# An attention and two expert layers on one core: where in SBUF the matmul operands lie, modulo 256 bytes

## The chip, the cores and the metric

The kernel runs on one core of one Trainium2 chip. The metric is the device time of one execution in microseconds (us). Three executions of the kernel before took 971.79, 973.72 and 978.30 us, median 973.72; the profiled execution took 974.34 us, of which its span from the first to the last instruction is 972.5 us, so 1.8 us lie around the span.

An SBUF address below is a byte offset inside a partition. "Residue" means that address modulo 256. For a pair of matmuls that follow each other, "offset" means the residue of the second one's weights (the stationary operand) less the residue of what the first one streams (the moving operand), modulo 256: it compares the two reads that TensorE makes at the same time.

## The reference

```python
def phi(x):                                  # q, k: (4, 8, 576, 64), omega: (128, 64)
    h = einsum('bhsd,md->bhsm', x, omega) - sum(x * x, -1) / 2
    return exp(h - max(h)) / sqrt(128)
kv, z = einsum('bhsm,bhsd->bhmd', phi(k), v), sum(phi(k), 2)
attn = einsum('bhsm,bhmd->bhsd', phi(q), kv) / (einsum('bhsm,bhm->bhs', phi(q), z) + 1e-6)
x = attn as (2304, 512)
x = (silu(x @ w_gate) * (x @ w_val)) @ w_out          # 512 -> 1536 -> 512, first expert layer
h = x @ w_in                                          # 512 -> 2048, second expert layer
g = where(h >= 1, h, where(h <= -1, 0, (h + 1)**2 / 4))
return g @ w_out2                                     # 2048 -> 512
```

All of it is float32; the expert weights arrive as 64-bit floats.

## The kernel before

**Products.** Each large product is made of three TensorE products of a high and a low part of both operands, so that 128x128 weights are loaded and 256 columns streamed three times for one result (`split3`, lines 397 to 400): L398 streams the high part, L399 the low part past the same weights, L400 the high part past the low part of the weights. 7,134 of the program's 7,782 matmuls stand on these three lines. Each tile that such a product reads holds the high part and, 2,048 bytes or a multiple of it behind, the low part, so both have one residue.

**Stages.** Up to about 250 us the attention runs (lines 605, 678, 763, 867, 875), mixed with the first steps of the first expert layer (`moe1`). From there to about 600 us the rest of the first expert layer runs, and after 600 us the second one. In both layers PE alternates between a few products of an *up* projection (`set_up`, `tail_up`: streamed is x, weights are w) and a few of a *down* projection. In the first layer's down projection (`out1`, `down1`) the activations `hl` are streamed past the weights; in the second layer's (`down2`, `down_end`) the activations `hl` are the stationary operand, and the weights `w` are streamed.

**Order.** A planner in the kernel (class `Planner`) simulates the engines with fixed costs and writes the order of all instructions at build time. Buffers of one role form a `Ring`; a process takes one with `Get`, and `pl.put` gives it back. The planner doesn't know addresses.

**Homes.** Tiles get their addresses in the order in which the pools hand them out, and `pad` puts unused bytes between them. `wring` holds the weight slots: 9 of the pool `keep` (`w`), later 8 of `rb` (`wb`) and 7 of `wl` (`wx`). `hrow` holds the activation rows `hl` and `hlr`. `x1s` and `xur` hold what the up products stream.

| operand | names in the rows | residue before |
|---|---|---|
| x of up products | x1s, xur | 160 |
| weights, of up and of down products | w, wb, wx | 224 |
| activations of down products | hl, hlr | 160 |
| attention | omr, omh, oml 224; ki, qi, vi, ebk, ebq, qtn, kvr, xhl 64; qt, kvz, ids 192 | mixed |

So the offset of neighbouring matmuls is 64 inside the up products and through the whole first expert layer; inside the second layer's down products it is 192; where that layer goes from an up to a down product or back it is 0; in the attention it is 0, 32, 96, 128, 160 or 192, by the pair (qt with kvz 0, omh with xhl 96).

Of the kernel before, what the change touches and what calls it, by code (L numbers as in the profile page):

```python
# [42 lines left out]
SLACK_D, SLACK_U = 3.0, 0.8  # L43

SLACK_A = 0.0

NATK = 3

# [232 lines left out]
def performer_moe_kernel(ctx: ExitStack, tc: tile.TileContext, qG, kG, om, ident,  # L281
# [10 lines left out]
    def ring(*a):  # L292
        return Ring(bufs(*a))
# [4 lines left out]
    keep = ctx.enter_context(tc.tile_pool(name="keep", bufs=1, side="left"))  # L298
    acc = []
    bank = ring(psum, "bank", 8, [P, 512])  # L300
    def pad(pool, name, nbytes):
        pool.tile([P, nbytes // 4], F32, name=name)

    pad(keep, "pad0", 352)
    wring = ring(keep, "w", 9, [P, 2, 512], F32R)
    wstage = ring(keep, "ws", N_WS, [P, 1024], U32)
    wtmp = ring(keep, "wt", 2, [P, 512])
    half = keep.tile([P, 1], F32, name="half")
# [16 lines left out]
    att = att_cm.__enter__()  # L325
    ebufs = {False: ring(att, "ebk", EBK, [P, 512]), True: ring(att, "ebq", EBQ, [P, 512])}
    kin = ring(att, "ki", KINS, [P, 512])
    vin = ring(att, "vi", VINS, [P, 576])
    qin = ring(att, "qi", QINS, [P, 512])
    lent_cm = tc.tile_pool(name="lent", bufs=1, side="left", reuse_waits="tile")  # L330
    lent = lent_cm.__enter__()
    lent_ids = set()
# [19 lines left out]
    lend(vin, "vl", N_VL, [P, 576])  # L352
    lend(qin, "ql", 2, [P, 512])
    lend(ebufs[False], "el", 2, [P, 512])
    nat_b = sorted({b for b in range(4) for k in range(NATK) if b * 576 < (k + 1) * TB and k * TB < (b + 1) * 576})
    kvr = {(b, d): att.tile([P, 2, 2, P], F32, name=f"kvr{b}_{d}") for b in nat_b for d in range(2)}
    qts0 = ring(att, "qtn", 3, [P, 2, TB])
    xhl = ring(att, "xhl", 2, [P, 2, 256], F32R)
    stat = ring(att, "st", 10, [P, 4, 4])
    rec = ring(att, "rec", 2, [P, TB])  # L360
    qts = ring(att, "qt", N_QT, [P, 2, 2, TB], F32R)
    kvz = [[att.tile([P, 2, 2, 2, P], F32R, name=f"kvz{b}_{d}") for d in range(2)] for b in range(2)]
    ids = att.tile([P, P], F32, name="ids")
    rect = ring(att, "rect", 1, [P, TB // 32, 33])
    nc.gpsimd.memset(rect.free[0][0][:, :, 32:33], 1e-6)
    omr = att.tile([P, 256], F32, name="omr")
    omh = att.tile([P, 256], F32R, name="omh")
    oml = att.tile([P, 256], F32R, name="oml")


    def dma(dst, src, nbytes):
# [52 lines left out]
        pl.put(wstage, st)  # L424
        return t

    def conv_key(key, src, slot):
        st = yield Get(wstage)
        pl.set(wdone[key])
        t = yield from to_f32(st, src, None)  # L430
        yield from parts(slot[:, 0], slot[:, 1], t, 512)
        pl.put(wtmp, t)
        wslot[key] = slot
        pl.set(wready[key])

    def conv(key, src, rng, prio):
# [2 lines left out]
        pl.spawn(conv_key(key, src, slot), prio)  # L439
        yield wdone[key]  # L440

    def wfree(key, rng):
        pl.put(rng, wslot.pop(key))

    moe_on = Ev()
    NE = N_EARLY[0]
# [55 lines left out]
    def w_feed():  # L502
        for m, a, order, sets in passes:
            for c in sets:
                for s, p in columns(m, c):
                    slots, tt = [], []
                    for i in range(2):
                        yield staged[s, 2 * p + i]
                    for _ in range(2):
                        tt.append((yield Get(wt2)))  # L510
                    for _ in range(4):
                        slots.append((yield Get(wring)))
                    pl.spawn(conv_pair(s, p, tt, slots), PR_W)
                for key in set_keys(m, c)[4:]:
                    yield staged[key]
                    t = yield Get(wt2)
                    slot = yield Get(wring)
                    pl.spawn(conv_one(key, t, slot), PR_W)

    def late_rank():  # L520
        return PR_C if moe_on.done else PR_CS
# [11 lines left out]
    def conv_pair(s, p, tt, slots):  # L533

        hs = [pl.spawn(dma(tt[i], w32[s, 2 * p + i], 262144), 0.6) for i in range(2)]
        for h in hs:
            yield h
        t0, t1 = tt
        lo, hi = slice(0, 256), slice(256, 512)
        yield from conv_slot((s, 2 * p), t0, slots[0])  # L540
        yield from conv_slot((s, 2 * p + 1), t1, slots[1])
# [4 lines left out]
        yield from conv_slot(("c" + s, p), t1, slots[2])  # L546
        pl.put(wt2, t1)
        yield from conv_slot(("d" + s, p), t0, slots[3])
        pl.put(wt2, t0)


# [376 lines left out]
    def att_close():  # L928
        for k in range(NBLK):
            yield x1_ready[k]  # L930
        att_cm.__exit__(None, None, None)
        rb = ctx.enter_context(tc.tile_pool(name="rb", bufs=1, side="right", reuse_waits="tile"))
        for rng, name, n, c in ((xpart, "xr", N_XR, [P, 512]), (ebr, "eb", N_EB, [P, 512]), (gbr, "gb", N_GB, [P, 1024]),
                                (wt2, "wtr", N_WT, [P, 512]), (hbuf, "hbr", N_HB, [P, 512]), (xq, "xq", N_XI, [P, 512])):
            for t in bufs(rb, name, n, c):
                pl.put(rng, t)
        for rng, name, n, more in ((hrow, "hlr", N_HL, 320), (wring, "wb", NB1, 192)):
            for t in bufs(rb, name, n, [P, 2, 512], F32R):
                pl.put(rng, t)
# [3 lines left out]
        pad(rb, "pad5", 320)  # L943
        pl.set(right_b)
        LEAN["DVE"], LEAN["POOL"] = LEAN_B, POOL_B

# [44 lines left out]
    def row_out(row, h):  # L991
        if len(row) > 2:
            if row[2] is not None:
                yield row[2]
        hl = yield Get(hrow)
        if len(row) > 2:
            pl.set(row[3])
        yield from parts(hl[:, 0], hl[:, 1], h, 512)
        pl.put(hbuf, h)
        row[1].append(hl)  # L1000
        pl.set(row[0])

    def evac1(k, d, last):
# [76 lines left out]
    def out1(step, h_ev, res):  # L1080
        k, fp = step
        first, last, end = run[step]
        for i in range(2):
            yield wready["o", 2 * fp + i]
        yield h_ev
        ws = [wslot["o", 2 * fp + i] for i in range(2)]
        hl = res[0]
        for n in range(KD):
            d, c = divmod(n, 2)
            if first and c == 0:  # L1090
                yield acc_free[d]
# [8 lines left out]
        pl.put(hrow, hl)  # L1100
        for f in (2 * fp, 2 * fp + 1):
            if last_use[f] == step:
                wfree(("o", f), wring)
# [155 lines left out]
    for m, a, order, sets in passes:  # L1259
        for j in order:  # L1260
            for c in sets:
                n = 2 if m == 1 and j < 4 else 1 if m == 1 else 4 if j < 4 else 2
                for r in range(n):
                    rows[m, a, j, c, r] = Ev(), [], before, Ev(), got, Ev()
                    before, got = rows[m, a, j, c, r][3], rows[m, a, j, c, r][5]

    def relu(dst, src, n):
# [310 lines left out]
    def late_down():  # L1578
        yield moe1_v
        yield from out1(*pend1.pop())  # L1580
        for m, a, order, sets in passes:
            for j in order:
# [14 lines left out]
                for i, (k, f, cols, end) in enumerate(todo):  # L1597
# [7 lines left out]
                    else:  # L1605
                        yield from (down1 if m == 1 else down2)(a, j, f, res[0], cols, i == 0, i == len(todo) - 1)
                    if end:
                        pl.put(hrow, res[0])
# [12 lines left out]

# [98 lines left out]
```

## Time and profile before

| | |
|---|---|
| median of three executions | 973.72 us |
| profiled execution, its span | 974.34 us, 972.5 us |
| PE busy, of the span | 958.3 us, 99% |
| DVE busy | 825.9 us, 85% |
| ACT busy | 567.4 us, 58% |
| POOL busy | 96.4 us, 10% |
| granted TensorE clock | full speed in every slice (2.4 GHz) |
| PE share of the chain that ended last | 62% |

Matmuls overlap in the records: one takes some 0.28 us from its issue to its end, and the next begins after 0.11 to 0.12 us. So PE counts as busy all the time, and what tells its pace is the distance of two starts, the *pitch*: a stretch without a wait, divided by its matmuls. The count of a window holds those that began before it and reach into it as well, so 2.5 (0.28 over 0.113) are taken off a count before dividing.

### The profile page before, as it was taken

To read this page: it belongs to the slowest core of one execution; us is meant where nothing else is said; L and a number is where in the kernel's file an instruction comes from. 1 tells how busy PE (TensorE), PEld (TensorE's weight loads), DVE (VectorE), ACT (ScalarE), POOL (GpSimd) and SP (SyncE) were. 2 spreads that over 40 slices of the span, in tenths; PEclk is the share of its full clock that TensorE was granted. 3 is DMA by queue.
4 is the path that set the end of the run, shared out by engine and by line. 5 is a ranking of instruction groups with operands and counts; after the bars stand their busy time and mean duration, and the time that the engine had idled before them with its cause. 6 is when DMAs were issued, how large, how long until landed. Compare 5 with 4: busy or idle time off the path is not lost.

```text
span 972.5 us, 21171 instructions
## 1 busy us (share of the span) xinstructions
PE 958.3 (99%) x8094; PEld 939.7 (97%) x8094; DVE 825.9 (85%) x1695; ACT 567.4 (58%) x1490; POOL 96.4 (10%) x99
## 2 busy tenths in 40 slices
PE   8999999999999999999999999999999999999998
PEld 6789999999999999999999999999999999999998
DVE  7999899888999999999999899899788768866553
ACT  8999788878645645445454566564445455544331
POOL 0332337434300000000000000000000000000000
PEclk9999999999999999999999999999999999999999
DMA  8766656635568465573657653445313041303022
GB/s 300 254 199 189 196 157 220 198 132 174 177 215 266 135 230 186 186 266 126 202 193 241 224 197 120 131 136 202 131 55 120 1 141 45 130 6 106 1 88 87
DMA packets 90677, 154.67 MB, mean 159 GB/s; under 512 B 8528, under 2 KB 42320, under 8 KB 90576
## 3 DMA queue, kind: packets, MB, share of 16 engines
q1 hardware_dynamic: 90576, 153.32, 48.2%
q8 instruction: 63, 1.03, 0.4%
q14 instruction: 38, 0.31, 0.1%
HBM read 110.30 MB, written 42.99 MB: 158 GB/s over the span
## 4 chain that ended last, share of the span: by engine, by line
PE 62%; DVE 11%; DMA 7%; ACT 4%; issue 2%; SPq 1%; POOL 0%; DVEq 0%; POOLq 0%; ACTq 0%
PE bank L398 20%; PE bank L400 20%; PE bank L399 20%; DMA ws<-in_wo_dram 2%; PE bank L875 2%; DMA ws<-in_w_dram 2%; DMA xq<-x1d 1%; DVE x1s L391 1%; DVE wt L422 1%; DVE wt L420 1%; DVE gb L1289 1%; DVE hb L1281 1%; DMA ki<-in_kG_dram 1%; PE bank L763 1%; PE bank L678 1%
## 5 line engine op out<-in xcount | busy, mean ns | idle before, releaser
L398 PE MATMUL bank<-x1s,w 128*128 128x256 f32 x492 | 139.0, 283 | 0.3 <-ACT eb L379 0.3
L400 PE MATMUL bank<-x1s,w 128*128 128x256 f32 x492 | 137.0, 278 | 0.0
L399 PE MATMUL bank<-x1s,w 128*128 128x256 f32 x492 | 136.9, 278 | 0.0
L398 PEld LDWEIGHTS bank<-x1s,w 128*128 128x128 f32 x492 | 92.8, 189 | 0.6 <-ACT eb L379 0.5
L400 PEld LDWEIGHTS bank<-x1s,w 128*128 128x128 f32 x492 | 92.6, 188 | 0.0
L399 PEld LDWEIGHTS bank<-x1s,w 128*128 128x128 f32 x492 | 92.5, 188 | 0.0
L379 ACT ACTIVATE x1s<-xq 128x512 fp32r<-128x512 f32 x81 | 50.8, 628 | 54.5 <-PE bank L400 35.0
L398 PE MATMUL bank<-x1s,wx 128*128 128x256 f32 x278 | 78.3, 282 | 2.3 <-ACT eb L379 1.8
L398 PE MATMUL bank<-x1s,wb 128*128 128x256 f32 x286 | 79.9, 279 | 0.0
L399 PE MATMUL bank<-x1s,wb 128*128 128x256 f32 x286 | 79.7, 279 | 0.0
L400 PE MATMUL bank<-x1s,wb 128*128 128x256 f32 x286 | 79.7, 279 | 0.0
L400 PE MATMUL bank<-x1s,wx 128*128 128x256 f32 x278 | 77.6, 279 | 0.0
L399 PE MATMUL bank<-x1s,wx 128*128 128x256 f32 x278 | 77.5, 279 | 0.0
L379 ACT ACTIVATE eb<-bank 128x512 f32<-128x512 f32 x95 | 56.1, 591 | 26.5 <-PE bank L400 26.0
L415 ACT ACTIVATE wt<-ws 128x512 f32<-128x512 f32 x68 | 45.9, 678 | 42.2 <-DMA ws<-in_w_dram 22.9
L391 DVE TENSOR_TENSOR x1s<-xq,x1s 128x512 fp32r<-128x512 f32 x90 | 61.7, 686 | 7.8 <-ACT x1s L379 7.4
L379 ACT ACTIVATE hlr<-hb 128x512 fp32r<-128x512 f32 x53 | 33.4, 631 | 52.7 <-PE bank L399 39.0
L398 PEld LDWEIGHTS bank<-x1s,wx 128*128 128x128 f32 x278 | 52.5, 189 | 3.3 <-ACT eb L379 2.6
L624 DVE TENSOR_REDUCE st<-bank 128x4 f32<-128x512 f32 x72 | 48.8, 684 | 7.7 <-PE bank L605 3.5
L1289 DVE TENSOR_TENSOR gb<-bank,eb 128x512 f32<-128x512 f32 x64 | 43.9, 686 | 12.3 <-PE bank L400 11.9
L398 PEld LDWEIGHTS bank<-x1s,wb 128*128 128x128 f32 x286 | 54.0, 189 | 0.2 <-DVE eb L1289 0.2
L400 PEld LDWEIGHTS bank<-x1s,wb 128*128 128x128 f32 x286 | 53.8, 188 | 0.0
(281 smaller groups left out, 3629.3 us busy)
## 6 DMA issues: line engine op xcount, KB each, us to landing
ws<-in_w_dram SPq DMA_DIRECT2D x40, 512.0 KB, 4.8
ws<-in_wo_dram SPq DMA_DIRECT2D x28, 512.0 KB, 5.3
xq<-x1d SPq DMA_DIRECT2D x36, 256.0 KB, 4.8
xq<-x2d SPq DMA_DIRECT2D x36, 256.0 KB, 3.9
qi<-in_qG_dram SPq DMA_DIRECT2D x34, 256.0 KB, 3.2
ki<-in_kG_dram SPq DMA_DIRECT2D x33, 256.0 KB, 3.5
vi<-in_kG_dram SPq DMA_DIRECT2D x28, 192.0 KB, 3.4
x1d<-os SPq DMA_DIRECT2D x18, 256.0 KB, 3.2
```

Source lines behind the costliest of these rows:

```text
L379: yield Op("ACT", c_act(n), lambda: nc.scalar.activation(dst, src, AF.Copy, scale=1.0 if scale is None else scale))
L391: yield Op("DVE", c_dve(n), lambda: nc.vector.tensor_tensor(out=dst, in0=a, in1=b, op=op), True)
L398: nc.tensor.matmul(ps, l_hi, r_hi, start=first, stop=False, skip_group_check=shared)
L399: nc.tensor.matmul(ps, l_hi, r_lo, start=False, stop=False, skip_group_check=shared)
L400: nc.tensor.matmul(ps, l_lo, r_hi, start=False, stop=last, skip_group_check=shared)
L415: yield Op("ACT", 0.575, lambda: nc.scalar.activation(t, hw.bitcast(F32), AF.Abs))
L420: yield Op("DVE", c_dve(512), lambda: nc.vector.scalar_tensor_tensor(out=ti, in0=lw, scalar=29, in1=ti, op0=ALU.logical_shift_right, op1=A ...
L422: yield Op("DVE", c_dve(512), lambda: nc.vector.scalar_tensor_tensor(out=ti, in0=hw, scalar=0xC0000000, in1=ti, op0=ALU.bitwise_and, op1=A ...
L624: yield Op("DVE", c_dve(512), lambda: nc.vector.tensor_reduce(out=st[:, :, 0], in_=psv, axis=AX.X, op=ALU.max, negate=True))
L678: nc.tensor.matmul(kp[:, 2 * pr + a], e[:, u * P:(u + 1) * P], vb[:, vi + (dv if li == 4 else 0), a * 64:a * 64 + P], start=(li == 0 and a ...
L875: nc.tensor.matmul(ps[:, a, c0:c1], kz[:, l, r, a], q_t[:, h, a, c0:c1], start=(l == 0 and h == 0), stop=(l == 1), skip_group_check=True)
L1289: yield Op("DVE", c_dve(512), lambda: nc.vector.tensor_tensor(out=dst, in0=pq(ps), in1=pq(e), op=ALU.add))
```

## The change

No instruction is added, removed or moved: on each of the five engines the built program holds the same instructions in the same order with the same operands. What differs is the addresses, and the waits of seven instructions (one of SP's DMAs `xq<-x1d`, the first into the later right-hand pool, now also waits for the last matmul of L875; four other DMAs of SP and two DVE instructions lose one wait each).

Tiles are put in another order with other pads. A weight slot becomes 1,088 floats long instead of 1,024, and a process places its 1,024 inside by role (`split_at`): weights of up products, and the early weights of the first layer's down products, at the slot's start (residue 224); later weights of the first layer's down products (`"o"`) 32 floats in (residue 96); those of the second layer's (`"p"`) 48 floats in (residue 160). The activation rows become one tile with views; the second layer's begin 48 floats in (residue 96), those of the first layer at 160 as before.

| pair: streamed, then weights | offset before | offset after |
|---|---|---|
| up, up | 64 | 64 |
| first layer: down, down (late) | 64 | 192 |
| first layer: up, down; down, up | 64; 64 | 192; 64 |
| second layer: down, down | 192 | 192 |
| second layer: up, down; down, up | 0; 0 | 192; 64 |
| attention's pairs | 0 to 192, mixed | 64 |

The residue of what is streamed: before 160, and 224 in the second layer's down products; after 160 everywhere in the table.

```diff
+O_OFF, P_OFF, H_OFF = 32, 48, 48
...
+    def split_at(t, off):
+        return t[:, off:off + 1024].rearrange("p (h c) -> p h c", h=2)
...
-    pad(keep, "pad0", 352)
-    wring = ring(keep, "w", 9, [P, 2, 512], F32R)
+    wring, hrow = Ring([]), Ring([])
+
+    def slot_tiles(pool, name, n):
+        for t in bufs(pool, name, n, [P, 1088], F32R):
+            pl.put(wring, t)
+
+    def row_tiles(pool, name, n):
+        t = pool.tile([P, 1024 * n + 48], F32R, name=name)
+        for i in range(n):
+            v = t[:, 1024 * i:1024 * i + 1072]
+            pl.put(hrow, v)
+
+    pad(keep, "pad0", 32)
+    x1_sets = ring(keep, "x1s", 3, [P, 2, KD, TB], F32R)
+    row_tiles(keep, "hl", 2)
...
-    pad(keep, "pad1", 160)
-    x1_sets = ring(keep, "x1s", 3, [P, 2, KD, TB], F32R)
     hbuf = ring(keep, "hb", 3, [P, 512])
-    hrow = ring(keep, "hl", 2, [P, 2, 512], F32R)
...
+    pad(keep, "pad1", 96)
+    slot_tiles(keep, "w", 9)
...
-    def conv_one(key, t, slot):
+    def conv_one(key, t, raw):
         yield from dma(t, w32[key], 262144)
-        yield from conv_slot(key, t, slot)
+        yield from conv_slot(key, t, split_at(raw, O_OFF if key[0] == "o" else P_OFF))
+        whole[key] = raw
         pl.put(wt2, t)
...
+        def up(key, t, raw):
+            whole[key] = raw
+            return conv_slot(key, t, split_at(raw, 0))
...
-        for rng, name, n, more in ((hrow, "hlr", N_HL, 320), (wring, "wb", NB1, 192)):
-            for t in bufs(rb, name, n, [P, 2, 512], F32R):
-                pl.put(rng, t)
-            pad(rb, "pad" + name, more)
-        for t in bufs(rb, "xur", N_XU, [P, 2, 2, TB], F32R):
+        row_tiles(rb, "hlr", N_HL)
+        pad(rb, "padj", 64)
+        xur = bufs(rb, "xur", N_XU, [P, 2, 2, TB], F32R)
+        pad(rb, "padk", 64)
+        slot_tiles(rb, "wb", NB1)
...
-        hl = yield Get(hrow)
+        raw = yield Get(hrow)
+        hl = split_at(raw, H_OFF if len(row) > 2 and row[6] == 2 else 0)
...
-        pad(wl, "pad2", 320)
-        for t in bufs(wl, "wx", NWL, [P, 2, 512], F32R):
-            pl.put(wring, t)
+        slot_tiles(wl, "wx", NWL)
```

Left out above: the attention's tiles, which are created in another order with one pad of 64 bytes, and the lines that hand the whole slot back to its ring (`whole`, `raw`).

## Rows read from the trace of the kernel before

**Rows 1.** The page: busy time by engine; the chain that ended last, by engine.

```profile
PE 958.3 (99%) x8094; PEld 939.7 (97%) x8094; DVE 825.9 (85%) x1695; ACT 567.4 (58%) x1490; POOL 96.4 (10%) x99
...
PE 62%; DVE 11%; DMA 7%; ACT 4%; issue 2%; SPq 1%; POOL 0%; DVEq 0%; POOLq 0%; ACTq 0%
```

**Rows 2.** Stretches: from:to, length, then PE, PEld, DVE, ACT, POOL busy (xcount).

```profile
0.00:250.00 250.00, 243.69 (x1933) 227.58 (x1934) 220.01 (x581) 213.18 (x840) 89.50 (x93) 1.00 0.63 201
250.00:425.00 175.00, 172.17 (x1497) 170.54 (x1496) 163.22 (x314) 89.34 (x167) 6.85 (x6) 1.00 0.63 207
425.00:492.00 67.00, 67.00 (x570) 67.00 (x570) 65.14 (x126) 35.82 (x68) 0.00 (x0) 1.00 0.57 187
492.00:554.00 62.00, 60.76 (x533) 60.36 (x532) 56.31 (x107) 30.43 (x57) 0.00 (x0) 1.00 0.60 198
554.00:600.00 46.00, 45.82 (x389) 45.62 (x389) 45.81 (x88) 29.64 (x56) 0.00 (x0) 1.00 0.60 206
600.00:770.00 170.00, 170.00 (x1462) 170.00 (x1462) 146.50 (x266) 88.41 (x161) 0.00 (x0) 1.00 0.34 112
770.00:820.00 50.00, 50.00 (x440) 50.00 (x439) 35.49 (x61) 24.13 (x44) 0.00 (x0) 1.00 0.27 90
820.00:972.00 152.00, 148.83 (x1285) 148.63 (x1284) 93.37 (x158) 56.43 (x99) 0.00 (x0) 1.00 0.21 67
```

**Rows 3.** Two stretches of the first expert layer without a wait, same columns.

```profile
330.00:390.00 60.00, 60.00 (x532) 60.00 (x531) 57.83 (x112) 28.61 (x54) 0.00 (x0) 1.00 0.56 185
430.00:490.00 60.00, 60.00 (x512) 60.00 (x511) 58.18 (x114) 32.24 (x62) 0.00 (x0) 1.00 0.56 184
```

**Rows 4.** One form of matmul in 330 to 390 us, then in 425 to 492 us.

```profile
L399 PE MATMUL bank<-x1s,wb 128*128 128x256 f32 x28 | 7.7, 276 | 0.0
...
L399 PE MATMUL bank<-x1s,wb 128*128 128x256 f32 x40 | 11.2, 281 | 0.0
```

**Rows 5.** PE in order of time: the first matmul of five blocks of six.

```profile
860.46 0.28 PE L398 MATMUL bank<-wx,hl 128*128 128x256 f32 x1
...
861.14 0.28 PE L398 MATMUL bank<-xur,w 128*128 128x256 f32 x1
...
861.85 0.28 PE L398 MATMUL bank<-wx,hl 128*128 128x256 f32 x1
...
862.56 0.28 PE L398 MATMUL bank<-xur,wx 128*128 128x256 f32 x1
...
863.25 0.28 PE L398 MATMUL bank<-w,hlr 128*128 128x256 f32 x1
```

**Rows 6.** PE in order of time around a wait; in brackets the idle time and releaser.

```profile
492.50 0.28 PE L399 MATMUL bank<-x1s,wb 128*128 128x256 f32 x1
492.62 0.28 PE L400 MATMUL bank<-x1s,wb 128*128 128x256 f32 x1
493.76 0.39 PE L398 MATMUL bank<-x1s,wx 128*128 128x256 f32 x1 [0.86 <-ACT eb L379]
...
494.56 0.28 PE L398 MATMUL bank<-x1s,wb 128*128 128x256 f32 x1
...
494.90 0.28 PE L398 MATMUL bank<-x1s,wb 128*128 128x256 f32 x1
```

**Rows 7.** PE's waits in 250 to 600 us: total us, times, longest.

```profile
PE bank L398 <- ACT eb L379: 2.1, 5, 0.9
PE bank L399 <- DVE hlr L391: 0.6, 1, 0.6
PE bank L399 <- DVE hl L391: 0.6, 1, 0.6
PE bank L398 <- DVE eb L1289: 0.5, 1, 0.5
PE bank L398 <- ACT hl L379: 0.4, 1, 0.4
```

**Rows 8.** Two forms in 0 to 250 us, then L875's last matmuls and SP's DMA.

```profile
L400 PE MATMUL bank<-x1s,w 128*128 128x256 f32 x168 | 46.8, 279 | 0.0
...
254.77 1.60 PE L875 MATMUL bank<-qt,kvz 128*128 128x256 f32 x12
...
266.35 0.48 SPq L372 DMA_DIRECT2D xq<-x1d  x1
```

More of the change, by code (lines that the diff above doesn't have):

```diff
@@ L322, in performer_moe_kernel @@
     xpart = ring(keep, "xp", 2, [P, 512])
+    pad(keep, "pad1", 96)
+    slot_tiles(keep, "w", 9)
     att_cm = tc.tile_pool(name="att", bufs=1, side="right", reuse_waits="tile")
     att = att_cm.__enter__()
+    stat = ring(att, "st", 10, [P, 4, 4])
+    rec = ring(att, "rec", 2, [P, TB])
+    rect = ring(att, "rect", 1, [P, TB // 32, 33])
+    vin = ring(att, "vi", VINS, [P, 576])
+    qts0 = ring(att, "qtn", 3, [P, 2, TB])
+    qts = ring(att, "qt", N_QT, [P, 2, 2, TB], F32R)
+    ids = att.tile([P, P], F32, name="ids")
+    omr = att.tile([P, 256], F32, name="omr")
+    omh = att.tile([P, 256], F32R, name="omh")
+    oml = att.tile([P, 256], F32R, name="oml")
+    pad(att, "pada", 64)
     ebufs = {False: ring(att, "ebk", EBK, [P, 512]), True: ring(att, "ebq", EBQ, [P, 512])}
     kin = ring(att, "ki", KINS, [P, 512])
-    vin = ring(att, "vi", VINS, [P, 576])
     qin = ring(att, "qi", QINS, [P, 512])
+    nat_b = sorted({b for b in range(4) for k in range(NATK) if b * 576 < (k + 1) * TB and k * TB < (b + 1) * 576})
+    kvr = {(b, d): att.tile([P, 2, 2, P], F32, name=f"kvr{b}_{d}") for b in nat_b for d in range(2)}
+    xhl = ring(att, "xhl", 2, [P, 2, 256], F32R)
+    kvz = [[att.tile([P, 2, 2, 2, P], F32R, name=f"kvz{b}_{d}") for d in range(2)] for b in range(2)]
     lent_cm = tc.tile_pool(name="lent", bufs=1, side="left", reuse_waits="tile")
@@ L354, in performer_moe_kernel @@
     lend(ebufs[False], "el", 2, [P, 512])
[L355 to L364, printed above, removed]
     nc.gpsimd.memset(rect.free[0][0][:, :, 32:33], 1e-6)
-    omr = att.tile([P, 256], F32, name="omr")
-    omh = att.tile([P, 256], F32R, name="omh")
-    oml = att.tile([P, 256], F32R, name="oml")
     def dma(dst, src, nbytes):
@@ L425, in to_f32, with conv_key @@
         return t
-    def conv_key(key, src, slot):
+    def conv_key(key, src, raw):
+        whole[key] = raw
+        slot = split_at(raw, 0)
         st = yield Get(wstage)
@@ L440, in conv @@
         yield wdone[key]
+    whole = {}
     def wfree(key, rng):
-        pl.put(rng, wslot.pop(key))
+        del wslot[key]
+        pl.put(rng, whole.pop(key))
     moe_on = Ev()
@@ L516, in w_feed @@
                     t = yield Get(wt2)
-                    slot = yield Get(wring)
-                    pl.spawn(conv_one(key, t, slot), PR_W)
+                    raw = yield Get(wring)
+                    pl.spawn(conv_one(key, t, raw), PR_W)
     def late_rank():
@@ L526, in conv_slot @@
         pl.set(wready[key])
-    def conv_one(key, t, slot):
+    def conv_one(key, t, raw):
         yield from dma(t, w32[key], 262144)
-        yield from conv_slot(key, t, slot)
+        yield from conv_slot(key, t, split_at(raw, O_OFF if key[0] == "o" else P_OFF))
+        whole[key] = raw
         pl.put(wt2, t)
     def conv_pair(s, p, tt, slots):
+        def up(key, t, raw):
+            whole[key] = raw
+            return conv_slot(key, t, split_at(raw, 0))
         hs = [pl.spawn(dma(tt[i], w32[s, 2 * p + i], 262144), 0.6) for i in range(2)]
@@ L539, in conv_pair @@
         lo, hi = slice(0, 256), slice(256, 512)
-        yield from conv_slot((s, 2 * p), t0, slots[0])
-        yield from conv_slot((s, 2 * p + 1), t1, slots[1])
+        yield from up((s, 2 * p), t0, slots[0])
+        yield from up((s, 2 * p + 1), t1, slots[1])
         yield from two(t1[:, hi], t1[:, lo], t1[:, hi], 256, ALU.add)
@@ L545, in conv_pair @@
         yield from two(t0[:, hi], t0[:, hi], t0[:, lo], 256, ALU.subtract)
-        yield from conv_slot(("c" + s, p), t1, slots[2])
+        yield from up(("c" + s, p), t1, slots[2])
         pl.put(wt2, t1)
-        yield from conv_slot(("d" + s, p), t0, slots[3])
+        yield from up(("d" + s, p), t0, slots[3])
         pl.put(wt2, t0)
@@ L936, in att_close @@
                 pl.put(rng, t)
-        for rng, name, n, more in ((hrow, "hlr", N_HL, 320), (wring, "wb", NB1, 192)):
-            for t in bufs(rb, name, n, [P, 2, 512], F32R):
-                pl.put(rng, t)
-            pad(rb, "pad" + name, more)
-        for t in bufs(rb, "xur", N_XU, [P, 2, 2, TB], F32R):
+        row_tiles(rb, "hlr", N_HL)
[3 more added lines that the diff above has]
+        slot_tiles(rb, "wb", NB1)
+        for t in xur:
             pl.put(xu, t)
-        pad(rb, "pad5", 320)
         pl.set(right_b)
@@ L1000, in row_out @@
         row[1].append(hl)
+        row[1].append(raw)
         pl.set(row[0])
@@ L1099, in out1 @@
                 pl.spawn(evac1(k, d, end))
-        pl.put(hrow, hl)
+        pl.put(hrow, res[1])
         for f in (2 * fp, 2 * fp + 1):
@@ L1263, in performer_moe_kernel @@
                 for r in range(n):
-                    rows[m, a, j, c, r] = Ev(), [], before, Ev(), got, Ev()
+                    rows[m, a, j, c, r] = Ev(), [], before, Ev(), got, Ev(), m
                     before, got = rows[m, a, j, c, r][3], rows[m, a, j, c, r][5]
@@ L1607, in late_down @@
                     if end:
-                        pl.put(hrow, res[0])
+                        pl.put(hrow, res[1])
                     if j == order[-1]:
```

## The prediction

> **What bounds the kernel.** I read the page first: PE is busy 99% of the span and has 62% of the chain that ended last [rows 1]. The clock is granted in full throughout, so a gain has to come from the pitch of the matmuls, from start to start, or from PE's waits. I then cut the span into stretches [rows 2] and divided each by its matmuls, less the 2.5 that straddle a window's edges. There the reader should see two paces. In 330 to 390 us, 60 us hold 529.5 matmuls, a pitch of 113.3 ns; in 430 to 490 us they hold 509.5, a pitch of 117.8 ns [rows 3]. No PE idles in either, the instructions are the same forms, and all offsets in both are 64. I call these the short and the long pitch; one matmul of the same form takes 276 ns in the first and 281 ns in the second [rows 4], so the duration alone tells which pitch a group ran in.
>
> Two more views tell what sets the pitch. Where the streamed residue never changes (the first expert layer), the pitch is kept over hundreds of matmuls and changes at a wait of PE: before 493 us the starts are 0.12 us apart, then PE idles 0.86 us, and after it three matmuls take 0.34 us, 113.3 ns each [rows 6]. Where it does change (the second layer, 160 in up products, 224 in down products), blocks of six follow each other at 0.68, 0.71, 0.71 and 0.69 us [rows 5]: short, long, long, and one that begins long and ends short. So going from up to down keeps the pitch, going from down back to up flips it, and the layer runs half and half. Four blocks take 2.79 us, 116.3 ns a matmul; the windows of that layer say 116.5 (170.00 us over 1,459.5), 114.3 (50.00 over 437.5) and 116.1 (148.83 over 1,282.5) [rows 2].
>
> **The change, part by part.** Instructions added, removed or moved: none, so DVE, ACT, POOL and the DMAs keep their work. Of the seven waits that differ, the one that is new could matter, since everything behind it on SP's queue would be late: the DMA xq<-x1d is issued at 266.35 us, and the last L875 matmul that it must now await ends at 254.77 + 1.60 = 256.37 us [rows 8]. Ten us of slack: nothing. The six lost waits gain nothing either, for the same reason: they belong to tiles of the same closed attention pool.
>
> The offsets are what is left. After the change all that is streamed has one residue, 160, so the streamed side no longer jumps at the blocks' borders; only the weights alternate, at 64 and 192. Both offsets allow the short pitch: an up block at 64 and a down block at 192 both ran at 113.3 ns (0.68 us is six of them) [rows 3, 5]. What is unknown is whether a border between 64 and 192, without the jump, keeps the short pitch, and whether it ends the long one. No row shows such a border. The nearest are the borders of the second layer: from short, up to down keeps it; from long, down to up ends it within one block (0.69 us) [rows 5]. The border that turns short into long, down to up, does so while the streamed residue goes back from 224 to 160, which is gone. I therefore take it that the short pitch survives and that the long one is ended at some border; the other ends are the rivals.
>
> The terms, against the profiled execution's 974.34 us (0.62 above the median of 973.72, within the spread of the three times, so I use the result for the median as it is):
>
> - *Second expert layer, 600 to 972 us.* At 113.3 ns its 1,459.5 + 437.5 + 1,282.5 matmuls take 165.4 + 49.6 + 145.3 us instead of 170.0 + 50.0 + 148.8: 8.5 us less. It is on the path: PE idles nowhere there before its end, and DVE is busy 86%, 71% and 61% of the three windows. The middle window already runs close to the short pitch without a wait, so I take off only 0.4 us for waits that come up (0 to 2): 8.1.
> - *First expert layer, 250 to 600 us.* The long stretches are 425 to 492 and 554 to 600 us. At 113.3 ns their 567.5 and 386.5 matmuls would take 64.3 and 43.8 us, 2.7 and 2.2 less. But nearly all of the layer's waits of 4.2 us [rows 7] lie in the short stretches: PE idles 2.83 + 1.24 us in their 237 us and 0.00 + 0.18 us in the long ones [rows 2]. At that rate, 1.7%, the 113 us would lose 1.9 again: 3.0 is the upper end. The lower end is DVE, which is busy 65.14 of 67 and 45.81 of 46 us: if its work can't move, 1.9 + 0.2 = 2.1 are left. I take 2.5, between the two, which are near each other.
> - *Attention, 0 to 250 us.* All offsets become 64. L400's matmuls average 279 ns [rows 8], some 60% of the way from 276 to 281. If all 1,930 matmuls of the window gained 60% of 4.5 ns, that were 5.2 us; the lower end is zero, since PE idles 6.3 us there, and DVE (220 us) and ACT (213) are busy 88% and 85% and hold PE back. I take 1.0, near the lower end, because about half of these matmuls stream 256 columns in this way and the evictions that PE waits for don't get faster.
>
> Sum: 8.1 + 2.5 + 1.0 = 11.6 us, 974.34 - 11.6 = 962.7 us.
>
> **The rivals.**
>
> *The pitch keeps itself, the long one too.* If a border of 64 and 192 changes nothing in either direction, then each stretch keeps what the last wait left, as the first layer does now. The second layer has no waits, so it would run nearly whole in one pitch: short 974.3 - 8.5 = 965.8, long 3,179.5 x 117.8 ns = 374.5 instead of 368.8, 980.0 us. For it: the first layer's long runs at constant residues. Against: in the second layer a long block did end at a border, and alternating weights disturb the long pitch twice in twelve matmuls.
>
> *The short pitch is lost at the borders (slower).* If a border from 192 back to 64 turns short into long, as the one with the jump does now, and nothing turns it back, the second layer costs 5.7 us more, and the first layer's short stretches, 1,494.5 + 530.5 matmuls, 4.5 ns each, 9.1 us, of which the 4.1 us of waits in them are given back; with 1.0 in the attention 974.3 + 5.7 + 5.0 + 1.0 = 986 us. It decides once less than half of the second layer's blocks run short. For it: the flip in rows 5, and that the first layer's down products now alternate as well, which they did not. Against: the flip goes with a jump of the streamed side that no longer exists.
>
> *Addresses do nothing.* Then the two pitches have another cause (a neighbour's traffic, the moment a wait ends), and the time stays at 974, between 971 and 978. For it: both pitches occur at one and the same offset, 64 [rows 3], and they change at waits [rows 6]. Against: the strict pattern by blocks in the layer whose residues alternate [rows 5]. The Trainium skill speaks for this rival (SBUF — State Buffer, "Who interferes with whom"): TensorE's two read ports, one for the moving operand and one for the weights, are independent, and it waits on nobody. By that rule the sum would be zero; that equal forms without a wait run 4% apart in this trace shows only that something else than ports in that simple sense is at work.
>
> **The numbers.** The forecast has 0.64; the pitch that keeps itself 0.18, half of it short and half long; the short pitch lost 0.10; nothing 0.08. The predicted time is the forecast's, 962.7 us. Its own range is 957 to 968: 957 if the first layer gives its whole 4.9 and the attention 3, 968 if DVE eats the first layer's gain and the second layer gets waits of 2 us and a block in four stays long (0.03 us for each of some 130 blocks, 4 us, in part). To hold 8 times in 10 the range has to take in the rival without effect as well, up to 978; the long half of the first rival and the slower one are left out. 957 to 978 us.
>
> A change of 1%, 9.7 us, is about what a measurement of this kernel can tell from none. Below 964.0 lies some 0.7 of the forecast and a third of the short half of the first rival: 0.48 faster. Above 983.5 lies most of the slower rival: 0.08. The rest, 0.44, is within 1%.
>
> **What would show it.** In the profile after, matmuls of L398 to L400 should average 276 to 277 ns instead of 278 to 283, in the first layer and in the second. Five successive blocks of the second layer should start 0.68 us apart, all of them. The windows from 600 us on should hold the same 3,180 matmuls in some 360.5 us. The first layer's waits should grow to 5 to 6 us, and PE's share should fall a little below 99%. If the second layer's blocks show 0.71 throughout, the pitch kept itself or was lost; if they still alternate, the streamed residue was not the cause. If they are short, but the span shrinks by less than 8 us, PE met a wait that its slower pace hid, and that wait stands in the list of waits after 600 us, where there is none now.

## The result and the profile after

The changed kernel takes 964.41 us (median of six executions, 962.18 to 966.87) against 975.68 us for the kernel before on the same chip (six, 970.94 to 981.42): a ratio of 0.988, 95% interval 0.985 to 0.991. The same kernel in a later job, six executions again, gave 964.15 us and a ratio of 0.989 (0.987 to 0.991). The profiled execution took 963.52 us, its span 961.7 us.

The page of the kernel after, its line of busy times and its chain by engine, answers to [rows 1]:

```profile
PE 945.6 (98%) x8094; PEld 927.5 (96%) x8094; DVE 824.1 (86%) x1695; ACT 567.1 (59%) x1490; POOL 96.8 (10%) x99
...
PE 64%; DVE 9%; DMA 7%; ACT 5%; issue 2%; SPq 1%; DVEq 0%; ACTq 0%
```

PE has the same 8,094 matmul records and is busy 12.7 us less; DVE, ACT and POOL differ by 1.8 us at most. The same stretches as in [rows 2] (from:to, length, then PE, PEld, DVE, ACT, POOL busy with counts, granted clock, DMA share, GB/s):

```profile
0.00:250.00 250.00, 243.30 (x1933) 227.25 (x1934) 219.85 (x581) 213.44 (x840) 89.91 (x93) 1.00 0.62 202
250.00:425.00 175.00, 172.94 (x1513) 172.07 (x1512) 164.75 (x317) 90.81 (x170) 6.85 (x6) 1.00 0.64 207
425.00:492.00 67.00, 64.22 (x562) 63.63 (x560) 64.58 (x125) 34.56 (x67) 0.00 (x0) 1.00 0.59 196
492.00:554.00 62.00, 61.06 (x531) 60.67 (x532) 56.41 (x107) 31.39 (x60) 0.00 (x0) 1.00 0.58 193
554.00:600.00 46.00, 46.00 (x406) 46.00 (x405) 45.72 (x88) 29.14 (x54) 0.00 (x0) 1.00 0.60 200
600.00:770.00 170.00, 170.00 (x1503) 170.00 (x1502) 148.47 (x270) 89.66 (x163) 0.00 (x0) 1.00 0.34 112
770.00:820.00 50.00, 50.00 (x444) 50.00 (x443) 38.42 (x68) 27.06 (x51) 0.00 (x0) 1.00 0.28 91
820.00:961.00 141.00, 138.05 (x1219) 137.85 (x1217) 85.92 (x145) 51.03 (x89) 0.00 (x0) 1.00 0.22 72
```

Read the counts, not the busy times. Up to 250 us there are 1,933 matmuls in both kernels: between these two profiles the attention gained nothing. From 250 to 600 us there are 3,012 instead of 2,989, 23 matmuls or 2.6 us more. In 600 to 770 us 170.00 us hold 1,500.5 instead of 1,459.5 (2.5 taken off each): 113.3 ns instead of 116.5. In 770 to 820 it is 441.5 instead of 437.5, 113.3 ns as well. Between identical matmuls of the two traces, the starts give 248.64 and 248.63 us for the attention, 349.97 and 347.37 for the first layer, 368.50 and 360.31 for the second: 0.0, 2.6 and 8.2 us, 10.8 in all.

The first matmul of five blocks of six in the second layer, PE in order of time, against [rows 5]:

```profile
860.64 0.28 PE L416 MATMUL bank<-x1s,w 128*128 128x256 f32 x1
...
861.33 0.28 PE L416 MATMUL bank<-w,hlr 128*128 128x256 f32 x1
...
862.00 0.28 PE L416 MATMUL bank<-x1s,wx 128*128 128x256 f32 x1
...
862.68 0.28 PE L416 MATMUL bank<-w,hlr 128*128 128x256 f32 x1
...
863.37 0.28 PE L416 MATMUL bank<-x1s,w 128*128 128x256 f32 x1
```

They lie 0.69, 0.67, 0.68 and 0.69 us apart, 2.73 us for four blocks where [rows 5] had 2.79: all short. From 602.7 us to the end all 3,132 distances from start to start are, with no other pace between.

The form of [rows 4], again in 330 to 390 and in 425 to 492 us (the line is L417 now; count, busy time, mean ns), and the one of [rows 8] in the attention:

```profile
L417 PE MATMUL bank<-x1s,wb 128*128 128x256 f32 x28 | 7.7, 276 | 0.0
...
L417 PE MATMUL bank<-x1s,wb 128*128 128x256 f32 x40 | 11.0, 276 | 0.0
...
L418 PE MATMUL bank<-x1s,w 128*128 128x256 f32 x168 | 46.7, 278 | 0.0
```

The second was 281: 425 to 492 us is short now. The attention's form only went from 279 to 278. PE's waits in 250 to 600 us (total us, times, longest), against [rows 7]:

```profile
PE bank L416 <- ACT eb L397: 2.8, 3, 2.5
PE bank L416 <- DVE eb L1318: 1.9, 2, 1.4
PE bank L417 <- DVE hlr L409: 0.8, 2, 0.5
PE bank L416 <- ACT hlr L397: 0.2, 1, 0.2
```

5.7 us instead of 4.2: what the pace gave here, the waits took in part. After 600 us the list of waits is empty, as before; a wait too short for it comes up under e1. Last, what a wait still does in this layer, PE in order of time (idle time and releaser in brackets):

```profile
553.55 0.39 PE L416 MATMUL bank<-x1s,wx 128*128 128x256 f32 x1 [0.15 <-ACT eb L397]
...
557.19 0.28 PE L416 MATMUL bank<-x1s,wb 128*128 128x256 f32 x1
...
557.89 0.28 PE L416 MATMUL bank<-hl,w 128*128 128x256 f32 x1
...
558.60 0.28 PE L416 MATMUL bank<-xur,wx 128*128 128x256 f32 x1
...
559.28 0.28 PE L416 MATMUL bank<-hl,w 128*128 128x256 f32 x1
```

A wait at 553.55 us leaves the long pitch behind: the last up block takes 0.70 us (557.19 to 557.89), the down block at offset 192 0.71, and the up block after it, back at 64, 0.68. The long pitch went into the down block and ended where the offset went from 192 to 64.

### The profile page after: what moved, and what is told of

Read it like the earlier page. It is cut to its first block, busy times and chain, and to the rows that moved or that the text cites. A ratio compares the mean times of both kernels' runs of the same rounds, so it can differ in the third digit from the quotient of the medians.

```text
span 961.7 us, 21166 instructions
## 1 busy us (share of the span) xinstructions
PE 945.6 (98%) x8094; PEld 927.5 (96%) x8094; DVE 824.1 (86%) x1695; ACT 567.1 (59%) x1490; POOL 96.8 (10%) x99
## 4 chain that ended last, share of the span: by engine, by line
PE 64%; DVE 9%; DMA 7%; ACT 5%; issue 2%; SPq 1%; DVEq 0%; ACTq 0%
PE bank L416 21%; PE bank L418 20%; PE bank L417 20%; DMA ws<-in_w_dram 2%; DMA ws<-in_wo_dram 2%; DMA xq<-x1d 2%; PE bank L902 1%; SPq L390 1%; DVE x1s L409 1%; DMA wtr<-w32o 1%; PE bank L705 1%; PE bank L790 1%; DVE wt L440 1%; ACT rec L838 1%; DVE wt L438 1%
## 5 line engine op out<-in xcount | busy, mean ns | idle before, releaser
L417 PE MATMUL bank<-x1s,w 128*128 128x256 f32 x492 | 136.2, 277 | 0.0
L417 PEld LDWEIGHTS bank<-x1s,w 128*128 128x128 f32 x492 | 92.5, 188 | 0.0
L417 PE MATMUL bank<-x1s,wb 128*128 128x256 f32 x286 | 79.0, 276 | 0.0
L417 PE MATMUL bank<-x1s,wx 128*128 128x256 f32 x278 | 76.8, 276 | 0.0
L416 PEld LDWEIGHTS bank<-x1s,wb 128*128 128x128 f32 x286 | 53.7, 188 | 0.1
L418 PEld LDWEIGHTS bank<-x1s,wb 128*128 128x128 f32 x286 | 53.7, 188 | 0.0
L417 PEld LDWEIGHTS bank<-x1s,wb 128*128 128x128 f32 x286 | 53.7, 188 | 0.0
```

The costliest lines, as they stand in the source:

```text
L416: nc.tensor.matmul(ps, l_hi, r_hi, start=first, stop=False, skip_group_check=shared)
L417: nc.tensor.matmul(ps, l_hi, r_lo, start=False, stop=False, skip_group_check=shared)
L418: nc.tensor.matmul(ps, l_lo, r_hi, start=False, stop=last, skip_group_check=shared)
```

## The experiments

The kernels e1 to e7 alter the three constants of the change, one or two lines, or both; the order of the instructions stays the same. The two bench kernels are programs of their own. `O_OFF` places the late down weights of the first layer, `P_OFF` the weights that the second layer's down products stream, `H_OFF` the `hl` that they hold as weights. The kernel before was run in the same jobs (medians 974.65, 977.33 and 974.51 us of 25, 3 and 11 executions; 972.27 us once).

**No border at all (e1_all64).** Every offset is 64 and every streamed residue 160.

```diff
-O_OFF, P_OFF, H_OFF = 32, 48, 48
+O_OFF, P_OFF, H_OFF = 0, 48, 16
```

> All pairs at offset 64, streamed residue 160 everywhere (the change without its 192). My theory: the pitch is kept at every border and a long one ends only by a border from 192 to 64, of which there is none now; so after each wait the pitch that the wait left stays, for tens of us in the first layer, and the whole second layer runs in one pitch: 962 to 967 us where that is the short one, 975 to 981 where it is the long one, and single runs differ by more than 8 us. Rival, that no offset of 0 is all that matters: 964 us like the change, blocks of 0.68 us.

Measured: 962.21, 964.30, 966.93, and 978.69, 980.50 us. The ratio of 0.990 (0.985 to 0.995) is that of the first three; two more single executions show that the last two belong to the kernel as well.

> The kernel of e1_all64 once more (every offset 64, no border between 64 and 192), a single execution with its profile, to see which pace its second layer has. Theory (at a constant offset the pace that the last wait left is kept to the next wait, and no wait comes in the second layer): the second layer, some 3,180 matmuls, runs nearly whole in one pace. Short gives 962 to 967 us with some 360 us from 600 us to the end, long 978 to 981 us with some 374 us; nothing between. Rival (the times of 978.7 and 980.5 of that kernel were disturbed executions, and the pace has nothing to do with them): the second layer is short in this one too, whatever the time, or short and long blocks mix.

> As e1_look1, a second single execution of the kernel with every offset 64. Theory: again one pace for the whole second layer, short with 962 to 967 us or long with 978 to 981 us, independent of what the first look shows. Rival: short whatever the time, or a mixture of short and long blocks with a time between.

Measured: 979.86 and 983.64 us. The window 600 to 770 us of the first e1 execution (962.21 us), of e1_look1 and of e1_look2:

```profile
600.00:770.00 170.00, 170.00 (x1503) 170.00 (x1502) 147.83 (x268) 89.57 (x163) 0.00 (x0) 1.00 0.34 112
```

```profile
600.00:770.00 170.00, 170.00 (x1446) 170.00 (x1445) 145.82 (x264) 88.15 (x160) 0.00 (x0) 1.00 0.34 112
```

```profile
600.00:770.00 170.00, 170.00 (x1448) 170.00 (x1447) 148.55 (x270) 91.97 (x169) 0.00 (x0) 1.00 0.36 119
```

One program, no idle time of PE in that window, the clock granted in full: 113.3 ns a matmul, or 117.8 and 117.6. The second layer takes 360.29, 374.42 and 374.26 us. In e1_look1 the long pitch began where PE was held up at 554.35 us, still in the first layer. e1_look2 shows the moment, in order of time:

```profile
607.67 0.59 ACT L397 ACTIVATE eb<-bank 128x512 f32<-128x512 f32 x1
...
608.27 0.28 PE L418 MATMUL bank<-hl,w 128*128 128x256 f32 x1
608.38 0.31 PE L416 MATMUL bank<-xur,wx 128*128 128x256 f32 x1
608.53 0.28 PE L417 MATMUL bank<-xur,wx 128*128 128x256 f32 x1
608.65 0.28 PE L418 MATMUL bank<-xur,wx 128*128 128x256 f32 x1
```

The matmuls up to 608.38 are short. One then takes 0.15 us to the next, 0.04 more than its neighbours, and the 3,136 distances behind it, to the end, are long. By its semaphore this matmul waits for the copy of ACT shown above, which ended some 0.1 us before it: a wait, but one that the idle time doesn't show, since the matmuls ahead still overlap it. In the first e1 execution the same copy ended 0.21 us before the same matmul, which went on without a stumble. So at one offset the pace keeps itself: the rival of that name is what happens without borders. The theory held, one pace for nearly the whole second layer, whichever, and 980.0 us, the rival's price for the long way, lies between the four measured.

The changed kernel meets the same stumble at the same matmul. In its second profile (after_again), in order of time:

```profile
600.79 0.59 ACT L397 ACTIVATE eb<-bank 128x512 f32<-128x512 f32 x1
...
601.49 0.34 PE L416 MATMUL bank<-xur,wx 128*128 128x256 f32 x1
601.66 0.28 PE L417 MATMUL bank<-xur,wx 128*128 128x256 f32 x1
...
602.25 0.28 PE L416 MATMUL bank<-hl,w 128*128 128x256 f32 x1
...
602.60 0.28 PE L416 MATMUL bank<-xur,wb 128*128 128x256 f32 x1
```

The copy ended some 0.1 us ahead, the matmul took 0.17 us to the next, and the long pitch came up. It was gone at 602.60 us, at the first step from 192 back to 64, after 7 long distances instead of 3,136.

**The second layer alone (e2_first64).** The first layer stays at 64 throughout.

```diff
-O_OFF, P_OFF, H_OFF = 32, 48, 48
+O_OFF, P_OFF, H_OFF = 0, 48, 48
```

> The first layer's down products back at 64, the second layer as in the change. My theory: the second layer runs short from its first border on (360 us for 3,180 matmuls); the first layer keeps a long pitch after some waits, 0 to 5 us lost, 964 to 970 us. Rival, that no offset of 0 is all that matters: 964 us, no long stretch in the first layer beyond one run of up products.

Measured: 965.8 us (nine executions, 963.36 to 969.87), ratio 0.992 (0.990 to 0.995). The profiled one, 969.87 us, in a stretch of the first layer and one of the second:

```profile
330.00:410.00 80.00, 80.00 (x681) 80.00 (x680) 74.56 (x141) 36.84 (x69) 0.00 (x0) 1.00 0.54 178
...
600.00:770.00 170.00, 170.00 (x1498) 170.00 (x1498) 149.71 (x273) 91.96 (x168) 0.00 (x0) 1.00 0.35 115
```

80.00 us over 678.5 are 117.9 ns: the first layer runs long for hundreds of matmuls. The second begins long and is short from 612.1 us on, soon after its first step from 192 to 64, with 3,105 matmuls to the end. Its 360.60 us are nearly the change's 360.31. The first layer takes 352.46 us in this profile.

**The first layer alone (e3_first_only).** The second layer as before.

```diff
-O_OFF, P_OFF, H_OFF = 32, 48, 48
+O_OFF, P_OFF, H_OFF = 32, 0, 0
```

> The first layer's down products at 192 as in the change, the second layer as before (offset 0 at its borders, streamed residue 224 in its down products). My theory: the second layer alternates again (0.68, 0.71, 0.71, 0.69 us a block), 8.3 us more than the change, 971 to 974 us; the first layer has no long stretch beyond a run of up products. Rival, that the attention and the first layer bring most of the gain: 966 us or less.

Measured: 973.13 us (ten, 970.93 to 975.43), ratio 0.999 (0.997 to 1.001).

```profile
600.00:770.00 170.00, 170.00 (x1464) 170.00 (x1464) 147.84 (x269) 89.44 (x164) 0.00 (x0) 1.00 0.35 113
```

116.3 ns, half short and half long, as before. The offsets of the first layer and the attention together give 1 us, between -1 and 3, in these executions; I had predicted 3.5 for them.

**Offsets 64 and 192, but a jump of the streamed side (e4_jump).** Streamed are 160 in up and 32 in down products; the offset-0 pairs of the kernel before are gone.

```diff
-O_OFF, P_OFF, H_OFF = 32, 48, 48
+O_OFF, P_OFF, H_OFF = 32, 16, 16
```

> All offsets 64 or 192, none 0, but the streamed residue of the second layer's down products is 32 instead of 160, so that it jumps by 128 at each border (up to down at 64, down to up at 192). My theory: the jump, not the offset 0, is what flips the pitch; blocks of the second layer are not all short, 3 to 16 us more than the change, 967 to 980 us. Rival, that no offset of 0 is all that matters: 964 us, blocks of 0.68 us throughout.

Measured: 973.91 us (ten, 970.26 to 977.29), ratio 1.001 (0.999 to 1.003). The first matmul of four blocks, PE in order of time:

```profile
860.86 0.28 PE L416 MATMUL bank<-wx,hl 128*128 128x256 f32 x1
...
861.57 0.28 PE L416 MATMUL bank<-xur,w 128*128 128x256 f32 x1
...
862.26 0.28 PE L416 MATMUL bank<-wx,hl 128*128 128x256 f32 x1
...
862.96 0.28 PE L416 MATMUL bank<-xur,wx 128*128 128x256 f32 x1
```

0.71, 0.69 and 0.70 us: neither pace holds. Offsets of 64 and 192 alone are not enough; with a jump of the streamed residue by 128 at every border their gain is gone.

**Roles exchanged (e5_swap).** Up weights at 192, down weights at 64.

```diff
-O_OFF, P_OFF, H_OFF = 32, 48, 48
+O_OFF, P_OFF, H_OFF = 0, 48, 16
...
-            return conv_slot(key, t, split_at(raw, 0))
+            return conv_slot(key, t, split_at(raw, 32))
```

> The roles exchanged: late up weights 192 behind what streams, late down weights 64, streamed residue 160. My theory: any border at which the weights' offset changes and the streamed residue doesn't is as good if the border from 192 to 64 is the one that ends a long pitch: second layer short, 964 us (962 to 968). Rival, that up products want 64 and down products 192: 968 us or more, with blocks of 0.71 us.

Measured: 966.76 and 964.93 us, ratio 0.988 (0.978 to 0.999). The second layer is short from end to end, 360.29 us: there it doesn't matter which product has which offset, only that both occur. The first layer took 351.54 us in this profile, 4 us more than in the change's two, with 7.5 us of waits and a moment at the lower clock (last section).

**Offset 0 (e6_zero).** The weights at the residue of what streams.

```diff
-O_OFF, P_OFF, H_OFF = 32, 48, 48
+O_OFF, P_OFF, H_OFF = 48, 48, 0
...
-            return conv_slot(key, t, split_at(raw, 0))
+            return conv_slot(key, t, split_at(raw, 48))
```

> All late weights of both layers at offset 0, streamed residue 160 (the first steps of the first layer and the attention stay at 64). My theory: one pitch of about 120 ns, as L875's pair at offset 0 shows now; some 6,000 matmuls at 6.7 ns more than the short pitch, less the waits of the first layer that vanish: 995 to 1005 us. Rival, that addresses don't matter beyond chance: 964 to 980 us.

Measured: 995.16 and 994.66 us, at the lower end of what I expected (one just below it), ratio 1.018 (1.007 to 1.029).

```profile
600.00:770.00 170.00, 170.00 (x1419) 170.00 (x1418) 144.96 (x263) 89.12 (x162) 0.00 (x0) 1.00 0.37 122
```

120.0 ns a matmul, in all but one of the 3,245 distances from 600 us on. Between this and the change lie 30 us, made by addresses alone.

**The paces by themselves (bench_pitch).**

> Only matmuls of the form of L398 (128x128 weights, 256 columns, float32r), 72 series of 49, each after a wait; nothing of the reference is computed. Series by the offset between streamed operand and next weights, with one residue for all that is streamed, and series in which the streamed residue steps on from matmul to matmul. [...] Rival, that only the offset counts: all series at offset 64 show 113.3 or 117.8 ns whatever the step.

Measured, mean pitch in ns once a series had settled: offset 0 120.0 in three of three; 32 118.3; 64 113.3 in two and 117.8 in one; 96 117.2 to 118.5; 128 118.7; 160 120.0; 192 117.8 in three of three; 224 116.7 to 117.8. With a streamed residue that steps from one matmul to the next (by 32 to 224, offset 64), 115.8 to 119.2; in the other series, where it alternates between two residues, 116.7 to 120.0. For steps of 128 I had expected 110.0; they ran at 116.7, and no series ran below 113.3. That only the offset counts is refuted as well: at offset 64 the step changes the pace.

**The steps by themselves (bench_step).**

> The kernel computes nothing of the reference: it only issues 55 series of 43 matmuls of one size (128 x 256, fp32r), each after a wait for ScalarE, with weights and streamed operands at addresses of my choice: eleven patterns, five series of each. A name gives the offset of the weights behind the streamed operand before them, in bytes modulo 256: 64_d_64 is 18 matmuls at 64, 6 at d, 18 at 64 (d = 0, 32, 96, 128, 160, 192, 224); 192_64 is 18 at 192, then 24 at 64; jump64, jump128 and jump192 stay at 64, but the streamed operand's residue moves by 64, 128 or 192 after 18. Theory (64 and 192 have each two stable paces; the step from 192 to 64 ends a long one, the step from 64 to 192 keeps what it finds): every series of 64_192_64 and 192_64 ends at 113.3 ns, whatever it began with; 64_0_64 runs at 120.0 ns in its six. jump128, which the kernel before does at each border, flips the pace: 113.3 ns ahead becomes 117.8 behind, and the other way round; jump64 and jump192 do not flip so cleanly. Rival (the pace behind a border is chance, and the changed kernel's second layer is lucky): the ends of 64_192_64 and 192_64 are short in some of five series and long in others, as the restarts of same64 were (2 and 1 of 3), and jump128 gives the same mixture. Which other d end a long pace I cannot derive; I take 96 and 128 as likely and 32 as unlikely.

The streamed residue stands still in the first seven patterns and in the last; all five series of a pattern agree (the very first series, 64_0_64, began at half the clock and is left out):

| pattern | pace ahead of the step, ns | pace at the end, ns |
|---|---|---|
| 64, six at 192, 64 | 113.3 | 113.3, also in the six |
| 192, then 64 | 117.8 | 113.3 |
| 64, six at 96, 128 or 160, 64 | 113.3 | 113.3, but 117 to 120 on average in the six |
| 64, six at 0, 32 or 224, 64 | 113.3 | 117.8 |
| 64 throughout, jump of 128 | 117.8 | 113.3 |
| 64 throughout, jump of 64 | 117.8 | 113.3 |
| 64 throughout, jump of 192 | 113.3 | 117.8 |

One series each of 192-then-64, 64-192-64 and 64-32-64, in groups of equal matmuls (start, us from the first start to the last end, count); less 0.28 us and divided by the count less one:

```profile
64.68 1.57 PE L330 MATMUL bank<-x,w 128*128 128x256 f32 x12
...
67.38 1.64 PE L330 MATMUL bank<-x,w 128*128 128x256 f32 x13
...
35.83 4.26 PE L330 MATMUL bank<-x,w 128*128 128x256 f32 x36
...
12.75 1.65 PE L330 MATMUL bank<-x,w 128*128 128x256 f32 x13
...
15.76 1.69 PE L330 MATMUL bank<-x,w 128*128 128x256 f32 x13
```

117, then 113; 114 right through the six at 192; 114, then 118. The two steps on which the change rests are no chance: 64 to 192 kept the short pitch five times in five, 192 to 64 ended the long one five times in five. It does so over a few matmuls: behind the step the distances were about 114, 117, 123 and 118 ns, then 113. A jump of the streamed residue at a constant offset changed the pace in all three patterns; each was seen from one side only (all series of a pattern began alike), so that the jump of 128 also turns short into long wasn't seen here.

**Steps inside the up products too (e7_mix), beside the change itself (after_again).**

```diff
-        slot = split_at(raw, 0)
+        slot = split_at(raw, O_OFF if key[1] % 2 else 0)
...
-            return conv_slot(key, t, split_at(raw, 0))
+            return conv_slot(key, t, split_at(raw, O_OFF if key[0][0] == "d" or key[0] in "gvi" and key[1] % 2 else 0))
```

> The change, and beside it the weights' offset alternates between 64 and 192 from one chunk to the next inside the up products too (odd chunks and the early ones lie 128 bytes further on), instead of only at the borders of a block. Theory (the step from 192 to 64 ends a long run, and nothing ends a short one): a long run that a wait in the first layer started ends at the next chunk, some 2 us later, not at the next border of a down block, some 5 us later; the changed kernel had about 1.0 us of long pace in the first layer and 0.02 in the second, so at most 1 us is to be had: 963.4 us, which can hardly be told from the change's 964.4. In the trace: in 250 to 600 us no long run of more than some 15 to 20 matmuls, where the changed kernel has runs of 40 to 46. Rival (the step ends a long pace only by chance, or also breaks a short one): long runs of 40 and more stay or appear in the second layer, and the time is 964 to 968 us.

> The changed kernel itself, unaltered, once more, as the measure on the same chip for e7_mix. Both theories: 964.4 us give or take 2, a ratio to the kernel before of 0.988 to 0.991.

Measured: 964.70 us (six, 962.48 to 965.37) beside 964.15 for the change: no difference. My bound on the runs failed: behind waits of the first layer five long runs of 23 to 40 matmuls stand. Of the steps from 192 to 64 that met the long pitch (those with five matmuls at the new offset behind them, without a wait), 8 of 13 ended it at once here, and 4 of 7 in e5; in the change's two profiles and e2's it was 8 of 8. Of the eight others, all three of e5 and two here ended it within the same block, over distances of about 116, 123 and 118 ns, as the measured series 192-then-64 did. Three, all of them here, left it standing for the whole block, and the next such step ended it. So the step ends the long pitch mostly, not always: 25 of 28. That the short pitch survives held everywhere: from 250 us on, in the profiles of the change (both), e2, e5 and e7, it went through some 1,500 steps from 64 to 192 and as many back without being lost once.

## Why the prediction came out

**The mechanism was right, and shown.** Of the two things that no row of before had, a border from 64 to 192 that keeps the short pitch and one from 192 to 64 that ends the long one, each is seen by itself in the measured series, and the second in the second layer of e2, which began long and turned short, and at the stumble of after_again. Standing still of the streamed side was the other half of the step: e4 took it away alone and the gain was gone. In all, 11.6 us were predicted; the medians of the same job differ by 11.3, the two profiles by 10.8.

**The second layer, 8.1 us predicted, 8.2 measured.** The terms were counts times 113.3 ns, and the layer takes 360.31 us where I wrote 360.5. I had taken off 0.4 us for waits that come up: the list shows none, and what came up is the stumble behind ACT's copy, under 0.1 us a profile. With the attention's offsets beside it, in e2, the layer is worth 7.5 us (a ratio of 0.9923 on 974.65).

**The first layer, 2.5 predicted, 2.6 between the two profiles, but not shown.** The waits grew to 5.7 us, as I had said (5 to 6). But e3 has these offsets too and gains 1 us, and the other profiles with the same first layer take 347.71 us (the change again), 350.89 (e4) and 352.16 (e3, some 3 of them from the lower clock of the last section) against 349.97 before. So that the two numbers agree is in part luck. What decides there is when DVE and ACT hand over, more than the pace: e1's short execution ran 417 to 490 us at the long pitch (619 matmuls) and took 346.38 us for the layer; e1_look1, short until 554 us but for one run of 35, took 349.55, with 6.9 us of PE's waits instead of 3.6. A faster PE arrives earlier at the same wait.

**The attention, 1.0 predicted, none shown.** The two profiles differ by 0.0 us, but the nine others with the same offsets up to there take 246.8 to 249.6 us against the one 248.64 before, so a gain of 1 us can't be told from none. The reading behind the upper end, 5.2 us, was wrong: I took the 279 ns of [rows 8] for a share of the long pitch, and with every offset at 64 it is still 278. Where offset 0 stood, the pace did improve: L875's products of 256 columns (L902 after) went from 283 to 278 ns, 0.4 us of busy time in all. PE's waits there grew by as much, from 6.3 to 6.7 us.

**The rivals.** *The pitch keeps itself* is what e1 does, at both prices that I had worked out (965.8 and 980.0; measured 962 to 967 and 979 to 984). The change escapes it only by its borders, and what these are worth is the certainty: e1's short executions are as fast as the change, and the changed kernel's twelve all lie between 962.18 and 966.87 us. *Short lost at the borders* did not come; in e4 the jump does this in part, at a ratio of 1.001. *Addresses do nothing* is refuted by e6. The Trainium skill (SBUF — State Buffer, "Who interferes with whom") says that PE never waits on anyone, and gives its read of the moving operand and its read of the weights a port each, independent of one another. Here 3,244 of 3,245 distances were 120.0 ns with both reads at one residue (e6) and 3,132 were 113.3 with 64 and 192 between them (the change), in the same order on a full clock: the measurement decides. Why the residue matters, and whether 256 bytes is the right unit, was not tested.

## What to carry to other kernels

Where PE never waits, divide a stretch's time by its matmuls before looking for anything else: two paces of equal instructions are a reason to look at the addresses. For products like these (128x128 weights loaded for each 256 columns), keep the streamed operand at one residue modulo 256 and let the weights lie 64 and 192 bytes further in turn, not 64 alone: the first recovered from a stumble in 25 of 28 steps, the second kept it to the next wait. Other shapes and types were not tried. Count the gain only in stages where PE is bound by nothing else; where another engine holds it back, a faster pace turns into waits.

## What was not expected of the hardware

- At offset 64 TensorE has two stable paces, 113.3 and 117.8 ns. A stumble of 0.04 us, behind a wait that the idle time doesn't show, decided between them for 3,136 matmuls, 14 us (e1_look2).
- Offset 0 costs 120.0 ns a matmul, 5.9% more than the best.
- After a longer wait PE can run at the lower clock for a moment. In e7's profile, the window 492 to 500 us (the column before the last two is the granted clock, 0.79):

```profile
492.00:500.00 8.00, 7.18 (x48) 7.18 (x49) 5.48 (x11) 4.95 (x10) 0.00 (x0) 0.79 0.45 168
```

PE in order of time:

```profile
492.82 0.39 PE L416 MATMUL bank<-x1s,wx 128*128 128x256 f32 x1 [1.93 <-ACT eb L397]
...
494.34 0.41 PE L416 MATMUL bank<-xur,w 128*128 128x256 f32 x1
494.55 0.41 PE L417 MATMUL bank<-xur,w 128*128 128x256 f32 x1
```

PE idles 1.93 us, starts again at the long pitch, and at 494.34 us matmuls come 0.21 us apart, at the lower of the two clock levels (1.2 GHz): 16 of them, which cost some 1.6 us. e5's profile shows the same at 494.5 us; e3's profile and e1_look2 show it near 495 us and once more near 317 us, some 3 us in all. That is most of the 5.2 us by which e1_look2's first layer is longer than e1_look1's, and more than the 1.3 us by which e3's is longer than e4's. Neither profile of the change shows it, though PE idles 2.47 us at the same place in the first of them: the wait alone doesn't decide.
